# The softmax's output, from sub-block nine on, is transposed by way of DRAM and VectorE instead of TensorE

## The chip, the core and the metric

The kernel runs on one core of one Trainium2 chip. The metric is the device time of one launch in microseconds (us), as the median of several runs. The engines are TensorE (PE, matmuls and transposes), VectorE (DVE), ScalarE (ACT), GpSimd (POOL) and SyncE (SP); the sixteen DMA engines move data between DRAM and the on-chip SBUF. Each engine takes its instructions strictly in the order in which they were emitted for it, and waits at an instruction until what it reads is there.

## What is computed

Windowed attention over 4 batches of 8 heads, 576 positions, 64 values per head, then two feed-forward layers over the 2304 tokens, all in float32:

```python
scores = scale * np.matmul(q, k.transpose(0, 1, 3, 2))
rel = pos[:, None] - pos[None, :]
scores = np.where((rel >= 0) & (rel < 64), scores, -1e9)
attn = np.exp(scores - np.max(scores, axis=-1, keepdims=True))
attn = attn / (np.sum(attn, axis=-1, keepdims=True) + 1e-09)
x = np.matmul(attn, v)                    # then heads side by side: [2304, 512]
h = x @ w1_in; g = np.maximum(h, 0.0)**2; x = g @ w1_out       # first layer
h = x @ w2_in                                                   # second layer
P = a[0] + a[1]*h + a[2]*h**2 + a[3]*h**3
Q = 1.0 + np.abs(b[0])*np.abs(h) + np.abs(b[1])*h**2
out = (P / (Q + 1e-06)) @ w2_out
```

## The kernel before

**Tiling.** The 2304 tokens are 18 sub-blocks of 128, called i = 0 to 17 here (sub-block nine is i = 8), and five blocks of 512 (the last has 256). Attention is done by sub-block, in two halves (gl = 0, 1) of 64 queries for each of 8 heads; the layers are done by block, in 16 steps j over the 2048 hidden columns. Every weight product is split into a high and a low part, so it needs three matmuls. A step has 12 matmuls into h (`h_mm`, L619), the activation (`mid1`: ScalarE's relu and squares, VectorE's subtraction into g at L692), and 12 matmuls of g into four accumulators (`out_mm`, L638), one step later.

**Where attention lies.** While the first layer works on block b, the sub-blocks of block b + 1 go through attention in slots between its matmuls: `q` and `k` (transposes of the inputs; from i = 12 on VectorE does them in 32x32 squares from data that was rearranged in DRAM, L463 and L485), `s` (the scores, L525, both halves, followed by `softmax`), `p` (the transposes of the softmax's output, one slot per half) and `x` (the values matmuls, L585). Scores of sub-block i + 1 and values of i are joined into one step on TensorE (`sx`).

**The route of a half.** VectorE masks the scores and takes the maximum (L542), ScalarE takes exponentials and sums (L547), VectorE inverts the sums (L551, L552) and multiplies (L555) into the tile `sm`. `slot_p` transposes `sm` on TensorE, four 128x128 pieces against the identity into PSUM (L568), and ScalarE or VectorE copies them into the tile `pT` (L573). The values matmuls read `pT` and v. There are two `sm` tiles and two `pT` tiles, used in turn.

**What sets the order.** Nothing is issued while the program is written: each piece is an `Item` with an assumed duration per engine, and `Plan.run` takes, one after the other, the item that can start earliest (ties by due time) and emits it. So an engine's order follows from the assumed durations, and from assumed gaps between engines (`Plan.gap`: 2000 ns after a DMA). Loads and stores are issued by SyncE (L319, `load`), all in one queue. GpSimd makes the masks and multiplies for i = 0 to 3, and after that does nothing.

## Time and profile before

| | us |
|---|---|
| median of 3 runs (lowest, highest) | 886.32 (885.85, 887.77) |
| the profiled execution | 890.21 |
| its span in the trace | 888.4 |
| TensorE busy | 870.5 |
| VectorE busy | 674.3 |
| ScalarE busy | 561.0 |
| GpSimd busy | 11.5 |

The profiled execution is one more run, with the profiler on; between its span and its time lie 1.8 us outside the trace. The first layer with the attention takes the first half of the span, the second layer the rest. In the profile's rows, "out<-in" are the names of the tiles, with their numbers left out, PEld is TensorE's loading of the stationary operand, and "idle before" is the time that the engine stood before the instruction, with the engine and line that let it go.

### The profile page before, as it was taken

The numbers are of one execution on the slowest core, as the hardware profiler recorded it, in microseconds if no ns is written. First come the engines' busy times: TensorE is split into PE (matmuls) and PEld (weight loads), VectorE is DVE, ScalarE is ACT, GpSimd is POOL, SyncE is SP. The second block draws the span as 40 slices with busy tenths as digits, with TensorE's granted clock in tenths as the row PEclk, the third lists the DMA queues.
The fourth block names the chain that finished last, engine by engine and source line by source line (L and its number), as shares of the span: only waits on it lengthen the run. The fifth ranks groups of instructions, "written<-read, shape, count | busy, mean of one in ns | idle before, by whom it ended". The sixth has DMA issues, their size and how long they took to land.

```text
span 888.4 us, 14088 instructions
## 1 busy us (share of the span) xinstructions
PE 870.5 (98%) x5152; PEld 726.5 (82%) x5152; DVE 674.3 (76%) x1435; ACT 561.0 (63%) x1172; POOL 11.5 (1%) x25
## 2 busy tenths in 40 slices
PE   7799999999999999999999999999999999999998
PEld 6678788888878888888899888888888888988886
DVE  6999995666466676754421899999999999999994
ACT  6778774656456554535444766676667667888764
POOL 4000000000000000000000000000000000000000
PEclk9999999999999999999999999999999999999999
DMA  9686662688855453633189910210011002100001
GB/s 230 187 243 199 188 192 84 200 219 220 223 179 184 147 184 141 238 134 126 49 313 372 361 45 0 96 48 1 1 47 48 1 1 94 49 1 24 1 1 48
DMA packets 152998, 113.64 MB, mean 128 GB/s; under 512 B 92769, under 2 KB 131681, under 8 KB 150881
## 3 DMA queue, kind: packets, MB, share of 16 engines
q1 hardware_dynamic: 152928, 112.75, 41.0%
q8 instruction: 40, 0.66, 0.3%
q14 instruction: 30, 0.24, 0.1%
HBM read 81.79 MB, written 34.08 MB: 130 GB/s over the span
## 4 chain that ended last, share of the span: by engine, by line
PE 88%; DVE 6%; DMA 3%; ACT 2%; issue 1%; SPq 0%; POOLq 0%; POOL 0%; ACTq 0%; DVEq 0%
PE h L619 30%; PE acc L640 22%; PE acc L638 19%; PE t L619 11%; PE t L525 1%; DMA raw<-in_moe_w_out_dram 1%; PE t L568 1%; DVE cvr L404 1%; PE h L585 1%; DVE cvr L407 1%; DVE sm L542 1%; DVE g L692 1%; DMA ld<-in_q_dram 0%; PE t L585 0%; DMA raw<-in_moe_w_in_dram 0%
## 5 line engine op out<-in xcount | busy, mean ns | idle before, releaser
L638 PE MATMUL acc<-g,wo 128*128 128x512 f32 (+1 forms) x960 | 215.9, 372 | 0.8 <-DVE g L692 0.8
L638 PEld LDWEIGHTS acc<-g,wo 128*128 128x128 f32 x960 | 167.3, 189 | 31.5 <-DVE g L692 1.4
L619 PE MATMUL h<-xh,wih 128*128 128x512 f32 (+1 forms) x480 | 181.1, 377 | 2.0 <-DVE rs L551 2.0
L619 PE MATMUL h<-xl,wih 128*128 128x512 f32 (+1 forms) x480 | 178.0, 371 | 0.3 <-DVE xl L603 0.3
L619 PE MATMUL h<-xh,wil 128*128 128x512 f32 (+1 forms) x480 | 178.3, 371 | 0.0
L619 PEld LDWEIGHTS h<-xh,wih 128*128 128x128 f32 x480 | 91.0, 190 | 18.0 <-ACT sm L547 2.1
L692 DVE TENSOR_TENSOR g<-cvr,g 128x512 fp32r<-128x512 f32 (+1 forms) x80 | 50.8, 635 | 71.7 <-ACT cvr L690 71.4
L619 PEld LDWEIGHTS h<-xh,wil 128*128 128x128 f32 x480 | 91.1, 190 | 16.0 <-DVE wil L419 0.4
L619 PEld LDWEIGHTS h<-xl,wih 128*128 128x128 f32 x480 | 91.1, 190 | 14.9 <-DVE xl L603 0.6
L685 ACT ACTIVATE cvr<-h 128x512 f32<-128x512 f32 (+1 forms) x80 | 44.3, 554 | 84.9 <-PE h L619 83.0
L640 PE MATMUL acc<-wo,cvr 128*128 128x512 f32 x384 | 93.1, 390 | 0.0
L640 PE MATMUL acc<-wo,g 128*128 128x512 f32 x384 | 93.1, 389 | 0.0
L640 PEld LDWEIGHTS acc<-wo,g 128*128 128x128 f32 x384 | 71.6, 188 | 14.6
L640 PEld LDWEIGHTS acc<-wo,cvr 128*128 128x128 f32 x384 | 71.5, 188 | 14.4
L736 DVE SCALAR_TENSOR_TENSOR kT<-kT,b,sm 128x512 f32<-128x512 f32 (+1 forms) x80 | 55.8, 698 | 16.4 <-ACT kT L731 13.8
L399 ACT ACTIVATE cvr<-raw 128x512 f32<-128x512 f32 x64 | 42.9, 671 | 30.3 <-DMA raw<-in_moe_w_out_dram 13.7
L738 ACT ACTIVATE raw<-kT,cb 128x512 f32<-128x512 f32 (+1 forms) x80 | 54.9, 686 | 8.8 <-DVE kT L736 6.6
L619 PE MATMUL t<-xl,wih 128*128 128x512 f32 (+1 forms) x160 | 58.9, 368 | 0.0
L619 PE MATMUL t<-xh,wil 128*128 128x512 f32 (+1 forms) x160 | 58.8, 368 | 0.0
L619 PE MATMUL t<-xh,wih 128*128 128x512 f32 (+1 forms) x160 | 58.8, 367 | 0.0
L749 DVE SCALAR_TENSOR_TENSOR pT<-pT,coef,raw 128x512 f32<-128x512 f32 (+1 forms) x80 | 55.8, 697 | 1.7
L740 ACT ACTIVATE raw<-raw,cb 128x512 f32<-128x512 f32 (+1 forms) x80 | 54.5, 681 | 1.7
(150 smaller groups left out, 1322.6 us busy)
## 6 DMA issues: line engine op xcount, KB each, us to landing
raw<-in_moe_w_in_dram SPq DMA_DIRECT2D x64, 256.0 KB, 3.4
raw<-in_moe_w_out_dram SPq DMA_DIRECT2D x32, 512.0 KB, 4.5
w2h_d<-raw SPq DMA_DIRECT2D x32, 256.0 KB, 2.1
w2l_d<-cvr SPq DMA_DIRECT2D x32, 256.0 KB, 2.1
ld<-in_v_dram SPq DMA_DIRECT2D x25, 256.0 KB, 3.9
out_dram<-ld SPq DMA_DIRECT2D x18, 256.0 KB, 2.1
x2h_d<-xh SPq DMA_DIRECT2D x4, 1024.0 KB, 5.1
x2l_d<-xl SPq DMA_DIRECT2D x4, 1024.0 KB, 7.7
```

What stands on the lines that cost most here:

```text
L399: plan.add({"act": act(DM)}, lambda e: A.activation(out=t.t, in_=raw.t.bitcast(F32)[:, :, 1], func=ACTF.Copy, scale=2.0 ** -112), [raw], [t])
L404: plan.add({"dve": dve(DM)}, lambda e: V.scalar_tensor_tensor(out=u(t), in0=u(t), scalar=3, in1=raw.t[:, :, 1], op0=ALU.logical_shift_left ...
L407: plan.add({"dve": dve(DM)}, lambda e: V.scalar_tensor_tensor(out=u(t), in0=raw.t[:, :, 0], scalar=29, in1=u(t), op0=ALU.logical_shift_rig ...
L619: T.matmul(out=v4(hp.t, n), lhsT=w.t[:, (c ^ 2) * 128:((c ^ 2) + 1) * 128], rhs=x.t[:, :n // 128, c, :], start=(c == 0 and z == 0), stop=( ...
L638: T.matmul(out=v4(acc[l, bi, m].t, n), lhsT=w.t[:, m, :], rhs=y.t[:, :n // 128, :], start=st, stop=en)
L640: T.matmul(out=v4(acc[l, bi, m].t, DM), lhsT=y.t[:, m, :], rhs=w.t, start=st, stop=en)
L685: plan.add({"act": act(n, True)}, lambda e: A.activation(out=r.t[:, :n], in_=hp.t[:, :n], func=ACTF.Relu), [hp], [r])
L692: plan.add({"dve": dve(n)}, lambda e: V.tensor_tensor(out=gl.t[:, :nq], in0=v4(r.t, n), in1=gh.t[:, :nq].bitcast(F32), op=ALU.subtract), [ ...
L736: plan.add({"dve": dve(n, ptr=1)}, lambda e: V.scalar_tensor_tensor(out=f(h2), in0=f(h2), scalar=b1, in1=f(ab), op0=ALU.mult, op1=ALU.add) ...
L738: plan.add({"act": act(n, ptr=1)}, lambda e: A.activation(out=f(y), in_=f(h2), func=ACTF.Ln, scale=2.0 ** -63, bias=cb[:, 0:1]), [h2], [y])
L740: plan.add({"act": act(n, ptr=1)}, lambda e: A.activation(out=f(y), in_=f(y), func=ACTF.Exp, scale=-1.0, bias=cb[:, 1:2]), [y], [y])
L749: plan.add({"dve": dve(n, ptr=1)}, lambda e: V.scalar_tensor_tensor(out=f(u), in0=f(u), scalar=coef[:, 0:1], in1=f(y), op0=ALU.subtract, o ...
```

## The change

From i = 8 on (`NPD`, the sub-blocks of the first two blocks) `slot_p` has no TensorE step and no PSUM tile. Instead, right after the multiplication, GpSimd issues a DMA that stores the half's [128, 512] tile into DRAM (`p_d`), and four DMAs that load it back into the same `sm` tile, so that partition 32 z + j holds key group z of query j of each 32. Now each 32x32 square only has to be transposed within itself, which VectorE does in one instruction into `pT`. For this the reductions, exponentials and multiplications of these sub-blocks write their tile in another layout (key group, head pair, 32 keys), and the values matmuls read their 64 columns as two pieces of 32. There are three `sm` tiles. An item can now carry its own gap (`lag`), and the two kinds of DMAs get durations on GpSimd of 1000 and 2500 ns and gaps of 3000 and 3500 ns.

```diff
@@ -42,6 +42,7 @@
         self.engines, self.emit, self.due = engines, emit, due
         self.deps, self.users = {}, []
         self.end = None
+        self.lag = None
 
 
 class Plan:
@@ -102,7 +103,8 @@
         def opened(it):
             it.ready = {}
             for e in it.engines:
-                it.ready[e] = max([d.end + self.gap(d.on, e) for d in it.deps], default=0)
+                it.ready[e] = max([d.end + (self.gap(d.on, e) if d.lag is None else d.lag) for d in it.deps],
+                                  default=0)
                 open_[e].append(it)
 
         for it in self.items:
@@ -176,6 +178,7 @@
     orders = (list(range(NB)), list(range(NB - 2)) + [NB - 1, NB - 2])
     NS0 = blocks[0][1] // 128
     NPE = sum(n for _, n in blocks[:3]) // 128
+    NPD = sum(n for _, n in blocks[:2]) // 128
     scale = 1.0 / float(D) ** 0.5
 
     ctx.enter_context(tc.manual_schedule())
@@ -194,7 +197,7 @@
     SMALL = [("cb", 2), ("coef", 6), ("na", 4), ("b1", 1)] + [(f"{x}{i}", 4) for x in ("nm", "su", "rs") for i in range(4)]
     TAGS = ([("ident", [128, 128], F32), ("mask", [128, 2, 128], F32)] +
             [(f"kT{i}", [128, HP, W + 128], F32) for i in range(2)] + [(x, [128, n], F32) for x, n in SMALL] +
-            [("pad", [128, 224], F32)] +
+            [("pad", [128, 208], F32)] + [("sm2", [128, 4, 128], F32)] +
             [(f"wi{x}{j}", [128, DM], F32R) for j in range(NF) for x in "hl"] +
             [(f"wo{j}", [128, KT, 2, 2, 128], F32R) for j in range(NF // 2)] +
             [(f"x{x}{i}", [128, 4, KT, 128], F32R) for i in range(2) for x in "hl"] +
@@ -232,6 +235,9 @@
     sq_d = {x: dram.tile([128, HP, (NSUB - NPE) * 4, 32], F32, name=f"{x}_squares_d") for x in "kq"}
 
 
+    p_d = dram.tile([NSUB - NPD, 2, 128, 4, 128], F32, name="p_d")
+
+
     turn = {}
 
     def buf(place, shape, dtype=F32, pool=sb, view=None):
@@ -255,7 +261,7 @@
 
     ALL_PS = ("t0", "h0", "t1", "h1", "acc0", "acc1", "acc2", "acc3")
     LD, RAW, CV = ring("ld", 6), ring("raw", 3), (0, 1, 2)
-    KTP, QTP, SM, PT = ring("kT", 2), ring("qT", 2), ring("sm", 2), ring("pT", 2)
+    KTP, QTP, SM, PT = ring("kT", 2), ring("qT", 2), ring("sm", 3), ring("pT", 2)
     shared = {}
 
     def part(place, tag, shape, dtype, view, gen=0):
@@ -313,11 +319,14 @@
 
     nat = {}
 
-    def load(dst, pieces, size, slow=1, reads=(), due=None):
+    def load(dst, pieces, size, slow=1, reads=(), due=None, own=None):
         def emit(_):
             for o, i in pieces():
-                nc.sync.dma_start(out=o, in_=i)
-        return plan.add({"dma": size / 360 * slow}, emit, reads, [dst], due)
+                (P if own else nc.sync).dma_start(out=o, in_=i)
+        it = plan.add({"pool": own[0]} if own else {"dma": size / 360 * slow}, emit, reads, [dst], due)
+        if own:
+            it.lag = own[1]
+        return it
 
     def toks(t0, n):
         done = 0
@@ -536,15 +545,25 @@
         sm[i, gl] = t
         kind = int((2 * i + gl) % GPB == 0)
         nm, su, rs = (buf(ring(x, 4), [128, 4]) for x in ("nm", "su", "rs"))
+        if i >= NPD:
+            keys = lambda x: x.rearrange("p (k j) -> p k j", j=32)
+            head = lambda c: t.t.rearrange("p k (h j) -> p k h j", j=32)[:, :, c, :]
+            full = lambda: t.t.rearrange("p k (h j) -> p k h j", j=32)
+            sums = lambda: rs.t.unsqueeze(1).unsqueeze(3).to_broadcast([128, 4, 4, 32])
+        else:
+            keys = lambda x: x
+            head = lambda c: t.t[:, c, :]
+            full = lambda: t.t
+            sums = lambda: rs.t.unsqueeze(2).to_broadcast([128, 4, 128])
 
         def top(_):
             for c in range(4):
-                V.tensor_tensor_reduce(out=t.t[:, c, :], in0=ps.t[:, c, :], in1=mask[:, kind, :], scale=-scale,
+                V.tensor_tensor_reduce(out=head(c), in0=keys(ps.t[:, c, :]), in1=keys(mask[:, kind, :]), scale=-scale,
                                        scalar=-NEG, op0=ALU.add, op1=ALU.min, accum_out=nm.t[:, c:c + 1])
 
         def exp(_):
             for c in range(4):
-                A.activation(out=t.t[:, c, :], in_=t.t[:, c, :], func=ACTF.Exp, scale=-1.0, bias=nm.t[:, c:c + 1],
+                A.activation(out=head(c), in_=head(c), func=ACTF.Exp, scale=-1.0, bias=nm.t[:, c:c + 1],
                              accum_out=su.t[:, c:c + 1])
 
         def norm(_):
@@ -552,16 +571,27 @@
             V.reciprocal(out=rs.t, in_=rs.t)
 
         def mul(e):
-            (P if e == "pool" else V).tensor_tensor(out=t.t, in0=t.t, in1=rs.t.unsqueeze(2).to_broadcast([128, 4, 128]),
-                                                    op=ALU.mult)
+            (P if e == "pool" else V).tensor_tensor(out=full(), in0=full(), in1=sums(), op=ALU.mult)
 
         plan.add({"dve": 850}, top, [ps], [t, nm])
         plan.add({"act": 1550}, exp, [nm, t], [t, su])
         plan.add({"dve": 350}, norm, [su], [rs])
         plan.add({"pool": 1400} if i < NS0 else {"dve": 690}, mul, [rs, t], [t])
+        if i >= NPD:
+            d = p_d[i - NPD, gl]
+            b = Buf(plan, f"p_d{i}{gl}", None)
+            load(b, lambda: [(d, t.t)], 1 << 18, reads=[t], own=(1000, 3000))
+            load(t, lambda: [(t.t[z * 32:(z + 1) * 32], d[:, z, :].rearrange("(a j) f -> j a f", j=32))
+                             for z in range(4)], 1 << 18, reads=[b], own=(2500, 3500))
 
     def slot_p(i, n, due):
-        src, ps = sm[i, n], ps_buf()
+        src = sm[i, n]
+        if i >= NPD:
+            t = pT[i, n] = buf(PT, [128, 4, 128])
+            plan.add({"dve": dve(512)}, lambda e: V.transpose(
+                t.t.rearrange("p a f -> p (a f)"), src.t.rearrange("p a f -> p (a f)")), [src], [t], due)
+            return
+        ps = ps_buf()
 
         def tr(_):
             for c in range(4):
@@ -585,7 +615,8 @@
                         T.matmul(
                             out=ps.t[e * 64:(e + 1) * 64, hp, gl * W:(gl + 1) * W],
                             lhsT=vg[gl].t[:, 2 * hp + e, :],
-                            rhs=pt[gl].t[:, hp, (e ^ gl) * 64:((e ^ gl) + 1) * 64],
+                            rhs=(pt[gl].t[:, (e ^ gl) * 2:(e ^ gl) * 2 + 2, hp * 32:(hp + 1) * 32] if i >= NPD else
+                                 pt[gl].t[:, hp, (e ^ gl) * 64:((e ^ gl) + 1) * 64]),
                             start=True, stop=True,
                         )
 
```

What the planner makes of it, at three places. Names before "<-" are written, names behind it read; numbers tell buffers apart.

TensorE, in the second block's steps at i = 13, before (h: `h_mm`, acc: `out_mm`, t from ident and sm: the transposes of the second half):

```order
L619 MATMUL h_3286<-xh_2107,wih_1117 128x512
L619 MATMUL h_3286<-xl_2114,wih_1117 128x512
L619 MATMUL h_3286<-xh_2107,wil_1124 128x512
L568 MATMUL t_3305<-ident,sm_3177 128x128 x4
L638 MATMUL acc_3031<-g,wo_1000 128x512 x3
L638 MATMUL acc_3039<-g,wo_1000 128x512 x3
L638 MATMUL acc_3044<-g,wo_1000 128x512 x3
L638 MATMUL acc_3050<-g,wo_1000 128x512 x3
```

and the same step now:

```order
L650 MATMUL h_3285<-xh_2122,wih_1119 128x512
L650 MATMUL h_3285<-xl_2135,wih_1119 128x512
L650 MATMUL h_3285<-xh_2122,wil_1126 128x512
L669 MATMUL acc_3019<-g,wo_1002 128x512 x3
L669 MATMUL acc_3026<-g,wo_1002 128x512 x3
L669 MATMUL acc_3032<-g,wo_1002 128x512 x3
L669 MATMUL acc_3051<-g,wo_1002 128x512 x3
```

The four transposes are gone, and the accumulating matmuls follow the step's last h matmul directly. Over the program TensorE has 2863 rows where it had 2883.

GpSimd, at the end of its work before (multiplications for i = 1 to 3, whose halves lie in weight tiles):

```order
L555 TENSOR_TENSOR wil_358<-wil_358,rs_412 128x512
L555 TENSOR_TENSOR wih_373<-wih_373,rs_453 128x512
L555 TENSOR_TENSOR wil_415<-wil_415,rs_487 128x512
L555 TENSOR_TENSOR wih_517<-wih_517,rs_557 128x512
L555 TENSOR_TENSOR wil_526<-wil_526,rs_585 128x512
L884 UNCONDITIONAL_BRANCH
L884 ISA
```

and now, the rows for i = 13 and 14 out of 40 new ones (p_d: the tensor in DRAM; x4: the four loads of a half):

```order
L325 DMA p_d<-sm_3167 128x512
L325 DMA p_d<-sm_3182 128x512
L325 DMA sm_3167<-p_d 32x4x128 x4
L325 DMA sm_3182<-p_d 32x4x128 x4
L325 DMA p_d<-sm_3399 128x512
L325 DMA p_d<-sm_3422 128x512
L325 DMA sm_3399<-p_d 32x4x128 x4
L325 DMA sm_3422<-p_d 32x4x128 x4
```

Both stores of a sub-block are issued ahead of both halves' loads; this is the order for all but i = 16, where the first half's loads stand ahead of the second store.

VectorE, after the multiplications for i = 13, before (raw, cvr: conversions of the second layer's weights; g: the activation's subtraction):

```order
L401 TENSOR_SCALAR raw_3246<-raw_3246 128x512
L404 SCALAR_TENSOR_TENSOR cvr<-cvr,raw_3246 128x512
L407 SCALAR_TENSOR_TENSOR cvr<-raw_3246,cvr 128x512
L419 TENSOR_TENSOR cvr<-cvr,raw_3246 128x512
L691 TENSOR_TENSOR cvr<-cvr 128x512
L401 TENSOR_SCALAR raw_3291<-raw_3291 128x512
L692 TENSOR_TENSOR g<-cvr,g 128x4x128
L404 SCALAR_TENSOR_TENSOR cvr<-cvr,raw_3291 128x512
L407 SCALAR_TENSOR_TENSOR cvr<-raw_3291,cvr 128x512
L419 TENSOR_TENSOR cvr<-cvr,raw_3291 128x512
```

and now:

```order
L410 TENSOR_SCALAR raw_3256<-raw_3256 128x512
L413 SCALAR_TENSOR_TENSOR cvr<-cvr,raw_3256 128x512
L416 SCALAR_TENSOR_TENSOR cvr<-raw_3256,cvr 128x512
L428 TENSOR_TENSOR cvr<-cvr,raw_3256 128x512
L591 STREAM_TRANSPOSE pT_3327<-sm_3167 128x512
L410 TENSOR_SCALAR raw_3294<-raw_3294 128x512
L723 TENSOR_TENSOR g<-cvr,g 128x4x128
L413 SCALAR_TENSOR_TENSOR cvr<-cvr,raw_3294 128x512
L416 SCALAR_TENSOR_TENSOR cvr<-raw_3294,cvr 128x512
L591 STREAM_TRANSPOSE pT_3348<-sm_3182 128x512
```

The two square transposes stand on both sides of a subtraction into g, 11 and 16 rows behind the second multiplication of the same sub-block, and wait there for the loads.

## Rows read from the trace of the kernel before

**Rows 1.** The page: span; busy us, share and instructions of each engine

```profile
span 888.4 us, 14088 instructions
PE 870.5 (98%) x5152; PEld 726.5 (82%) x5152; DVE 674.3 (76%) x1435; ACT 561.0 (63%) x1172; POOL 11.5 (1%) x25
```

**Rows 2.** The page: chain that ended last, by engine, then by line

```profile
PE 88%; DVE 6%; DMA 3%; ACT 2%; issue 1%; SPq 0%; POOLq 0%; POOL 0%; ACTq 0%; DVEq 0%
PE h L619 30%; PE acc L640 22%; PE acc L638 19%; PE t L619 11%; PE t L525 1%; DMA raw<-in_moe_w_out_dram 1%; PE t L568 1%; DVE cvr L404 1%; PE h L585 1%; DVE cvr L407 1%; DVE sm L542 1%; DVE g L692 1%; DMA ld<-in_q_dram 0%; PE t L585 0%; DMA raw<-in_moe_w_in_dram 0%
```

**Rows 3.** Stretches: length, busy PE PEld DVE ACT POOL, clock, DMA share, GB/s

```profile
145.00:258.00 113.00, 110.83 (x727) 90.22 (x726) 72.05 (x189) 66.16 (x167) 0.00 (x0) 0.99 0.71 194
258.00:346.00 88.00, 88.00 (x585) 71.98 (x584) 54.71 (x141) 48.63 (x115) 0.00 (x0) 0.99 0.59 192
```

**Rows 4.** By line, 145:440 us, PE: count, busy us, mean ns, idle

```profile
L568 PE MATMUL t<-ident,sm 128*128 128x128 f32 x80 | 12.0, 272 | 2.1 <-DVE sm L555 2.1
```

**Rows 5.** Timeline, PE, around one slot: start us, us, what

```profile
219.78 0.39 PE L619 MATMUL h<-xh,wil 128*128 128x512 f32 x1
220.02 0.60 PE L568 MATMUL t<-ident,sm 128*128 128x128 f32 x4
220.37 0.48 PE L619 MATMUL h<-xh,wih 128*128 128x512 f32 x1
220.69 0.40 PE L619 MATMUL h<-xl,wih 128*128 128x512 f32 x1
```

**Rows 6.** Timeline, PE: twelve weight matmuls, then scores and values

```profile
216.61 2.88 PE L638 MATMUL acc<-g,wo 128*128 128x512 f32 x12
219.33 0.39 PE L619 MATMUL h<-xh,wih 128*128 128x512 f32 x1
...
268.67 1.10 PE L525 MATMUL t<-kT,qT 64*64 64x128 f32 x32
269.70 1.15 PE L585 MATMUL h<-pT,ld 128*64 128x64 f32 x32
```

**Rows 7.** Instructions by line, whole span, DVE, shapes apart

```profile
L401 DVE TENSOR_SCALAR raw<-raw 128x512 uint32<-128x512 uint32 x64 | 27.1, 424 | 20.1 <-ACT cvr L399 19.6 <-DMA ld<-in_v_dram 0.3 <-DMA w2h_d<-raw 0.2
L692 DVE TENSOR_TENSOR g<-cvr,g 128x512 fp32r<-128x512 f32 x64 | 44.0, 688 | 36.8 <-ACT cvr L690 36.6
L463 DVE STREAM_TRANSPOSE qT<-ld 128x512 f32<-128x512 f32 x6 | 4.3, 710 | 3.9 <-DMA ld<-q_squares_d 3.9
L483 DVE COPY kT<-kT 128x256 f32<-128x256 f32 x6 | 1.7, 280 | 0.0
```

**Rows 8.** Timelines, DVE and PE: a subtraction and the matmuls that read it

```profile
300.84 0.69 DVE L692 TENSOR_TENSOR g<-cvr,g 128x512 fp32r<-128x512 f32 x1
...
302.64 0.62 PE L638 MATMUL acc<-g,wo 128*128 128x512 f32 x2
```

**Rows 9.** Timeline, DVE: the multiplications of the scores of 268.67

```profile
275.46 0.65 DVE L555 TENSOR_TENSOR sm<-sm,rs 128x512 f32<-128x512 f32 x1
...
276.90 0.69 DVE L555 TENSOR_TENSOR sm<-sm,rs 128x512 f32<-128x512 f32 x1
```

**Rows 10.** DMA issues: engine, count, KB each, median us from issue to landing

```profile
w2h_d<-raw SPq DMA_DIRECT2D x32, 256.0 KB, 2.1
...
ld<-q_squares_d SPq DMA_DIRECT2D x6, 256.0 KB, 3.2
```

**Rows 11.** Timeline, SP: four DMA issues in a row

```profile
130.72 2.54 SPq L319 DMA_DIRECT2D k_squares_d<-in_k_dram  x4
```

**Rows 12.** Timeline, POOL: its last operation

```profile
26.55 1.04 POOL L555 TENSOR_TENSOR wil<-wil,rs 128x512 f32<-128x512 f32 x1 [0.59 <-DVE rs L552]
```

**Rows 13.** Timeline, PE: the wait before a slot

```profile
255.76 0.63 PE L568 MATMUL t<-ident,sm 128*128 128x128 f32 x4 [2.10 <-DVE sm L555]
```

**Rows 14.** Stretches behind that wait, columns as in rows 3

```profile
256.00:258.00 2.00, 2.00 (x9) 1.67 (x8) 1.97 (x6) 1.57 (x3) 0.00 (x0) 0.63 0.00 0
258.00:260.00 2.00, 2.00 (x6) 1.54 (x5) 2.00 (x4) 1.85 (x4) 0.00 (x0) 0.51 0.92 385
```

## The prediction, made before the changed kernel was run

> **What bounds the kernel now.** I read the table of busy times first, then the chain of work that ended last, then the stretches of the stage that changes, and there the timelines. TensorE is busy 98% of the span, VectorE 76%, ScalarE 63%, GpSimd 1% [rows 1]. The chain runs 88% through TensorE, and the transposes that the change removes (L568) have 1% of it, weight matmuls 30, 22 and 19% [rows 2]. What matters is that TensorE has nearly no holes where the change acts: of 145 to 258 us it works 110.8 of 113, of 258 to 346 all 88, while VectorE has a third of each stretch free (72.1 and 54.7 us busy) [rows 3]. An instruction taken off TensorE there is therefore worth its own length, and a wait put on TensorE costs its own length. No other engine's busy time counts, only whether it delivers late.
>
> **What goes.** For i = 8 to 17, ten sub-blocks with two halves each, 20 slots of four transposes leave TensorE (80 instructions, x80 in [rows 4]). Their busy time, 12.0 us, is an upper bound, for matmuls overlap. What a slot costs is read from the spacing around it: the last matmul before it starts at 219.78 and the second one after it at 220.69, 0.91 us for two matmuls which elsewhere stand 0.2267 apart (twelve from 216.61 to 219.33) [rows 5, 6]. So a slot costs 0.91 - 0.45 = 0.46 us, and 20 slots **9.2 us**. That is the gain, if nothing else arrives late. The 20 evictions of PSUM go too; they lie on ScalarE and VectorE beside TensorE, so I count nothing.
>
> **What comes, off the path.** VectorE gets 20 square transposes at 0.71 us [rows 7], 14.2 us, covered by its idle third; where the cover is gone, one of them delays the g subtraction behind it (L692). The tightest such place I found has 0.69 us of subtraction from 300.84 and its matmul at 302.64, 1.1 us of slack [rows 8], so one transpose that does not wait for its data fits. The transfers add 20 times 512 KB of write and read, on DMA engines that are 0.71 and 0.59 busy [rows 3]. Reductions, exponentials and values matmuls now walk in pieces of 32 elements; no row shows these pieces. Zero is my value, since the weight matmuls also read x in pieces and keep their pace; a doubled values step (1.15 us, ten times, [rows 6]) is the far end, 11.5 us, and I give it almost no chance.
>
> **What comes, on the path.** A half's route is now: multiply (L555), store, four loads, square transpose, values matmul. TensorE meets the values at a place fixed by the order, and behind them, in order, stand all weight matmuls. So the sum is a race between two lengths.
>
> Available. In the changed order 81 to 87 weight matmuls lie between scores i and values i for i = 8 to 15, against 75 to 96 before. Take 84 at 0.2267: 19.0 us. With the scores itself (1.03, from 268.67 to 269.70), the previous values (1.15) and the next scores (1.03) [rows 6] that is 22.2 us; for i = 11 and 15 no scores follow, 21.2. The first multiply ends 7.4 us after the scores start (275.46 + 0.65 against 268.67) [rows 6, 9]. What is left is **14.8 us** for six sub-blocks, 13.8 for two. For i = 16 and 17 there are 189 and 120 matmuls, 43 and 27 us, and no race.
>
> Needed. GpSimd issues store 0, store 1, loads 0 (four), loads 1 (four) in this order, so from the first multiply to the second half's data pass one store issue, a landing, eight load issues and a landing. The second store's issue falls into the first one's landing; the second multiply ends 1.5 us after the first [rows 9]. A 256 KB store lands in 2.1 us, a 256 KB load of 32-wide squares in 3.2 [rows 10], and the transpose takes 0.71. Sum: 9c + 6.0 us, where c is what GpSimd needs for one DMA. No row shows c. Nearest from below is the same operation on SyncE: four issues in 2.54 us, 0.63 each [rows 11]; nearest from above is GpSimd's own 128x512 operation, 1.04 us [rows 12]. With 0.63 the need is 11.7 us, with 1.04 it is 15.4. I take the lower part, since SyncE's row is the same work on another engine, and then nobody waits: margin 3.1 and 2.1 us. At the upper end six sub-blocks wait 0.6 and two 1.6 us, together 6.8, and 2.4 us of gain are left.
>
> The Trainium skill, "DMA: Bandwidth & Descriptors", section "Latency and other measured facts", puts the first byte of a GpSimd-issued DMA at about 1 us and of one from SyncE at about 0.6. By that page each of the two landings would be some 0.4 us later, an estimate: the need 12.5 us, still inside. No run here shows it yet.
>
> **A wait that may go.** At 255.76 TensorE stood 2.10 us for the multiply of i = 12, directly before the removed transposes [rows 13], and then had a granted clock of 0.63 and 0.51 for four microseconds, the lower of its two levels (1.2 of 2.4 GHz) for most of them [rows 14]: another 0.43 x 4 = 1.7 us. So 3.8 us hang on it. The order removes the waiting instruction, but the block's eviction and g subtraction stand in the same VectorE queue at 254 to 258 us and would be late next. Bounds 0 to 3.8; I take zero, as the next waiter needs the same VectorE work.
>
> **Sum.** The profiled execution took 890.21 us for a span of 888.4; it lies 3.9 above the median of the three runs, 886.32. The change is a difference within the span, -9.2 + 0 = -9.2, so against the median the forecast is **877.1 us**. With the boundary wait gone wholly it would be 873.3; with c at its upper row 883.9.
>
> **Rivals.** (A) GpSimd is slow at issuing. The mechanism is the race above, its place the values of i = 8 to 15. It turns into a loss where the waits eat 9.2 us: 6x + 2(x + 1) = 9.2, x = 0.9, so c = (14.8 + 0.9 - 6.0)/9 = 1.08 us, hardly above GpSimd's row of 1.04. At c = 1.2 the need is 16.8: six waits of 2.0 and two of 3.0, 18 us, net +8.8, **895 us**; if each of them costs the clock as the one at 255.76 did, eight times 1.7 more, 909. For it: GpSimd issued no DMA before, and its rows are the slowest of all engines for their size. Against it: nothing in the trace says that an issue costs as much as an elementwise operation.
>
> (B) VectorE holds GpSimd off. VectorE has operations that run in a faster form: 512 elements in 0.424 us (L401) where L692 takes 0.69, and a copy of 256 in 0.28 [rows 7]. Between the first multiply and the second transpose of i = 13 the order has two of L401's and one copy, 1.1 us. If GpSimd stands still for them the need is 12.8 to 16.5 us: nothing at the lower end, 1.7 and 2.7 us at the upper one, 15.6 in all, net +6.4, **893 us**. The Trainium skill, "SBUF — State Buffer", section "SBUF: two separate sides", speaks of this against the change: while VectorE runs in a two-port mode, GpSimd cannot write descriptors, and such a DMA waits. By that rule the answer is (B); whether these rows are such a mode, and whether it matters, no run here shows yet.
>
> (C) The gain is given back through VectorE's queue. The first transpose of a half stands before a g subtraction and cannot be overtaken. Its data need 5c + 5.3 us from the multiply, 8.5 to 10.5. The rows between hold some 6.5 us of VectorE work and two subtractions, which TensorE's step spaces 5.4 us apart (24 matmuls), so they pass after 6.5 to 9 us. A wait of 2 us in each of eight sub-blocks would leave 0.9 beyond the 1.1 us of slack, 7.2 in all: **884 us**. That the change does not do what it says is out: the order has 20 rows fewer on TensorE.
>
> **How the numbers follow.** Forecast (873 to 882): 0.50, because the lower price is the like operation. (C), 882 to 888: 0.20. (A): 0.23, since its point of decision is so near to GpSimd's own row. (B): 0.07. A measurement of this kernel tells 0.2%, 1.8 us, from no change. Faster by more: all of the forecast and 0.11 of (C), 0.61. Slower by more: 0.21 of (A) and 0.06 of (B), 0.27. Between: 0.12. The range goes from the boundary wait gone, 873, up into (A) as far as c of about 1.2 with part of the clock's cost, 902; about 0.04 lie below it and 0.11 above.
>
> **What would show it.** Right: no transposes on TensorE between 145 and 440 us, TensorE with no waits at the values line, GpSimd's eight loads of a pair within 5 to 8 us, the stage from 145 to 440 shorter by 9 us and the rest alike. (A): waits of TensorE on the transpose line or of VectorE on the loaded tile, equal in every sub-block from 8 to 15, and a granted clock below 1 after them. (B): issue times on GpSimd that differ with what VectorE runs. (C): the g subtraction as TensorE's waited-for line. The forecast is wrong above all if c is over 1.08 us, which only the result can tell.

## The result: 0.6% slower, though the gain is there

| | before | changed |
|---|---|---|
| median of 7 runs, us | 886.55 | 892.17 |
| lowest to highest | 885.85 to 888.02 | 888.73 to 894.55 |
| profiled execution; its span | 890.21; 888.4 | 894.55; 892.3 |

The ratio is 1.0057, with a 95% interval of 1.0038 to 1.0076: 5.1 us slower, 3.4 to 6.7. The forecast was 877.1; the range, up to 902, took the time in, but the direction was wrong.

The page of the changed kernel, as [rows 1]: TensorE's busy time fell by 4.1 us and the span grew by 3.9, so that TensorE now stands still for 892.3 - 866.4 = 25.9 us instead of 17.9.

```profile
span 892.3 us, 14161 instructions
PE 866.4 (97%) x5072; PEld 722.1 (81%) x5072; DVE 682.5 (76%) x1450; ACT 552.9 (62%) x1157; POOL 67.8 (8%) x125
```

The stretches of [rows 3], with the same columns (length, busy PE PEld DVE ACT POOL, granted clock, DMA share, GB/s). Before, TensorE worked 110.83 and 88.00 us of them; the DMA share was 0.71 and 0.59:

```profile
145.00:258.00 113.00, 107.61 (x681) 86.62 (x680) 72.49 (x189) 60.21 (x155) 22.49 (x41) 0.97 0.84 232
258.00:346.00 88.00, 84.18 (x550) 68.39 (x550) 60.47 (x153) 46.96 (x112) 22.56 (x40) 0.98 0.71 217
```

TensorE's timeline there and up to 445 us, its six longest waits (start, us, instruction, [idle before <- releaser]): four values matmuls, at i = 10, 11, 12 and 15, wait for a square transpose (L591), and two groups of out matmuls for a g subtraction. At i = 8, 9, 13, 14, 16 and 17 the values do not wait.

```profile
211.42 1.03 PE L615 MATMUL h<-pT,ld 128*64 128x64 f32 x28 [1.41 <-DVE pT L591]
228.94 2.80 PE L669 MATMUL acc<-g,wo 128*128 128x512 f32 x11 [0.89 <-DVE g L723]
236.43 1.76 PE L615 MATMUL t<-pT,ld 128*64 128x64 f32 x28 [2.24 <-DVE pT L591]
276.10 1.14 PE L615 MATMUL h<-pT,ld 128*64 128x64 f32 x28 [2.29 <-DVE pT L591]
343.52 1.03 PE L615 MATMUL t<-pT,ld 128*64 128x64 f32 x28 [1.10 <-DVE pT L591]
384.92 2.81 PE L669 MATMUL acc<-g,wo 128*128 128x512 f32 x11 [1.22 <-DVE g L723]
```

The two waits over 2 us, at i = 11 and i = 12, are followed by the lower clock level (0.50), as the one of [rows 13, 14] was. Stretches of two microseconds, columns as above:

```profile
237.00:239.00 2.00, 2.00 (x26) 1.79 (x23) 0.77 (x2) 1.25 (x2) 0.00 (x0) 0.50 0.77 220
239.00:241.00 2.00, 2.00 (x6) 1.52 (x6) 1.88 (x4) 0.89 (x2) 0.00 (x0) 0.50 0.76 226
...
278.00:280.00 2.00, 2.00 (x6) 1.51 (x6) 2.00 (x15) 1.55 (x5) 0.00 (x0) 0.50 0.57 161
```

Who is late? GpSimd's instructions by line (count, busy us, mean ns, idle before) and the DMA issues of the page (KB each, median us from issue to landing), the latter as [rows 10]:

```profile
L325 POOL DMA_DIRECT2D sm<-p_d x80 | 44.9, 565 | 35.6 <-DMA p_d<-sm 32.0 <-DVE cvr L428 1.5 <-issue 1.0
```

```profile
w2h_d<-raw SPq DMA_DIRECT2D x32, 256.0 KB, 3.4
...
p_d<-sm POOLq DMA_DIRECT2D x20, 256.0 KB, 3.9
sm<-p_d POOLq DMA_DIRECT2D x80, 64.0 KB, 4.3
```

GpSimd issues a DMA in 0.56 us, below my lower bound of 0.63. The landings are late: 3.9 us where I had taken 2.1, 4.3 where I had 3.2. SyncE's own transfers land later too: the w2h_d store of [rows 10] went from 2.1 to 3.4 us.

Not every wait for a square transpose is a wait for a landing. At i = 10, 12 and 15 VectorE itself stood for the loaded tile before the second transpose (2.08, 3.40 and 1.75 us). At i = 11 it did not. It stood for ScalarE, which had stood 3.17 us for one of SyncE's raw loads, and came to the second transpose through its other work without a pause (timeline, DVE):

```profile
232.02 0.43 DVE L410 TENSOR_SCALAR raw<-raw 128x512 uint32<-128x512 uint32 x1 [3.14 <-ACT cvr L408]
...
235.67 0.70 DVE L591 STREAM_TRANSPOSE pT<-sm 128x512 f32<-128x512 f32 x1
```

From 145 to 445 us TensorE waits 10.3 us in all. Of these, 1.41 + 2.29 + 1.10 = 4.8 ended with a landing of the new transfers; the other 5.5 did not.

### The profile page after: what moved, and what is told of

It reads as the page before. It is cut to its first block, busy times and chain, and to the rows that moved or that the text cites. A ratio compares the mean times of both kernels' runs of the same rounds, so it can differ in the third digit from the quotient of the medians.

```text
span 892.3 us, 14161 instructions
## 1 busy us (share of the span) xinstructions
PE 866.4 (97%) x5072; PEld 722.1 (81%) x5072; DVE 682.5 (76%) x1450; ACT 552.9 (62%) x1157; POOL 67.8 (8%) x125
## 4 chain that ended last, share of the span: by engine, by line
PE 58%; DMA 2%; ACT 1%; DVE 1%; issue 0%; SPq 0%; ACTq 0%; DVEq 0%
PE acc L671 22%; PE h L650 17%; PE t L650 11%; PE acc L669 7%; DMA raw<-in_moe_w_in_dram 1%; DMA raw<-in_moe_w_out_dram 1%; DMA sm<-p_d 0%; ACT sm L566 0%; PE t L615 0%; PE t L534 0%; DVE g L723 0%; ACT raw L427 0%; SPq L325 0%; PE h L615 0%; DVE xl L738 0%
```

## The experiments

The kernel before took 886.6 to 889.4 us in the groups of runs, so all times below are ratios to it within the group, turned into us at 886.5; "changed" is +5.1. A difference between two rows carries the uncertainty of both, some 2 to 3 us.

| kernel | difference, us | 95% interval |
|---|---|---|
| changed | +5.1 | +3.4 to +6.7 |
| no transfers | -9.8 | -12.2 to -7.3 |
| SyncE's traffic cut | -10.4 | -12.3 to -8.4 |
| two of SyncE's stores cut | -1.1 | -2.4 to +0.4 |
| transfers, nobody waits | -2.8 | -4.0 to -1.7 |
| gaps of 5000 and 6000 | +11.9 | +9.7 to +14.2 |
| all gaps as measured | -0.4 | -1.6 to +0.9 |
| without i = 11, 12 | +2.7 | +1.4 to +3.8 |
| only i = 16, 17 | -0.1 | -1.3 to +1.2 |
| i = 12 to 17 | +1.1 | -0.1 to +2.2 |
| i = 12 to 17, gaps as measured | -3.6 | -4.9 to -2.4 |
| before, with a gap of 3500 | -1.1 | -2.1 to -0.1 |

**Is the gain there?** The transfers are left out.

```diff
-            for o, i in pieces():
+            for o, i in pieces() if not own else ():
...
```

> The changed kernel without GpSimd's transfers (the store to p_d and the four loads of each half are left out, so the squares are transposed without having been rearranged). Every other engine has the instructions of the changed kernel in the same order. Theory (the gain of 9.2 us is there and is eaten by transfers that land too late, and by the clock behind the waits): no wait of TensorE for VectorE's square transpose (L591), 875 to 879 us, that is 8 to 11 below the kernel before, and the other DMAs land as in the kernel before. Rival (the gain never was there, because pieces of 32 elements in softmax and values, or the changed order, cost it): 887 us or more, as slow as the changed kernel to within 4 us.

Measured: 878.23 us, -9.8. The theory holds for the time. The page shows 5072 matmuls and transposes, as in the changed kernel, but less busy time (9.6 us less, at a mean granted clock of 1.000 instead of 0.990; 1.5 of these lie before 145 us, where no transfer runs yet) and 7.6 us less idleness.

```profile
span 875.1 us, 13926 instructions
PE 856.8 (98%) x5072; PEld 715.9 (82%) x5072; DVE 682.2 (78%) x1450; ACT 553.0 (63%) x1157; POOL 11.5 (1%) x25
```

One wait for a square transpose is left, 1.32 us, again at i = 11, although nothing is transferred. It was not expected. Here too VectorE had stood 2.95 us for ScalarE, and ScalarE 2.97 us for a raw load:

```profile
229.91 1.03 PE L615 MATMUL t<-pT,ld 128*64 128x64 f32 x28 [1.32 <-DVE pT L591]
```

So more than half of the changed kernel's 2.24 us at i = 11 belongs to the new order, not to the transfers. SyncE's stores land nearly as before for w2h_d (2.3 us), later for w2l_d (3.1 instead of 2.1).

Two more things can be read. The pieces of 32 elements cost nothing: an exponential takes 389 ns in the median before and after the change, a multiplication 684 and 683, the values matmuls of a sub-block 1.15 us. And VectorE's busy time, 682.2 us here against 682.5 in the changed kernel, shows that GpSimd's issues do not slow it.

**Is it SyncE's traffic, or GpSimd's way of issuing?** SyncE's loads and stores for the second layer's weights become slivers.

```diff
+                f = 16 if l and j > 1 else 256
+                return [(o[:, c ^ 2:(c ^ 2) + 2, :f], i[:, c:c + 2, :f]) for c in (0, 2)]
...
-                load(w2_b[j, io, x], lambda p=p, d=d: [(d[io, j], p().bitcast(F32))], 1 << 18, reads=[b], due=due)
+                load(w2_b[j, io, x], lambda p=p, d=d, f=16 if j > 1 else DM: [(d[io, j][:, :f], p().bitcast(F32)[:, :f])], 1 << 18, reads=[b], due=due)
...
```

> The changed kernel with all its transfers on GpSimd and the same order on the compute engines, but SyncE's traffic cut: for the conversion of the second layer's weights (from its third tile on) only slivers of 16 or 32 columns are loaded and stored, and the second layer reads one stored tile again and again, so its result is not the layer's. Theory (GpSimd's transfers land late because they share the sixteen DMA engines with SyncE's stores and loads): store and loads of a half land in 2.0 to 2.7 us instead of 3.9 and 4.3, VectorE's waits for the loaded tile vanish, and the time is 875 to 881 us. Rival (a DMA that GpSimd issues lands late by itself): landings stay near 4 us, the waits of 2.2 us at i = 11 and i = 12 stay, 888 us or more.

Measured: 878.24 us, -10.4, with all of GpSimd's transfers in place. The time came out as the theory had it, the landings not quite: 3.1 us each in the median, still above the 2.7. TensorE's only wait for a square transpose between 145 and 445 us is one of 1.1, once more at i = 11. No run cut this traffic in the kernel before, so the time by itself does not say how much of the gain SyncE's own shorter traffic makes.

The transfers by themselves, in a kernel of their own:

> The transfers by themselves: a 256 KB store to DRAM and four loads of 64 KB of 32-wide squares, four times each (1) issued by GpSimd with nothing beside, (2) by SyncE with nothing beside, (3) by GpSimd while SyncE streams 512 KB loads, (4) by SyncE while ScalarE streams the same loads. Nothing of the reference is computed. Theory (shared DMA engines): alone both engines land in 2.0 to 2.5 us for the store and 2 to 3.2 us for the loads, equal to 0.4 us; beside the stream both are longer by 1.5 us or more. Rival (GpSimd's own DMAs are slow): phase 1 is longer than phase 2 by 1.5 us or more on each landing.

DMA issues of its four phases in order (engine's queue, count, KB each, median us to landing): alone by GpSimd and by SyncE, then beside a stream, by GpSimd and by SyncE.

```profile
pd<-half POOLq DMA_DIRECT2D x4, 256.0 KB, 2.3
half<-pd POOLq DMA_DIRECT2D x16, 64.0 KB, 2.2
...
pd<-half SPq DMA_DIRECT2D x4, 256.0 KB, 2.0
half<-pd SPq DMA_DIRECT2D x16, 64.0 KB, 2.0
...
pd<-half POOLq DMA_DIRECT2D x2, 256.0 KB, 5.8
half<-pd POOLq DMA_DIRECT2D x8, 64.0 KB, 5.7
...
half<-pd SPq DMA_DIRECT2D x16, 64.0 KB, 3.8
pd<-half SPq DMA_DIRECT2D x3, 256.0 KB, 6.0
```

Alone, GpSimd's transfers land 0.3 and 0.2 us later than SyncE's; beside a stream both need 1.8 to 4.0 us more, whoever issues them. Alone, then, the engine that issues hardly counts; what the DMA engines already have to do counts. (The loads' 5.7 against 3.8 us beside the stream do not compare the two engines: the stream kept the DMA engines full in the third phase, but only 0.5 to 1.0 busy in stretches of the fourth.) The Trainium skill, "DMA: Bandwidth & Descriptors", section "Latency and other measured facts", gives a memory latency of 0.2 us on average and 2 us at high load, as the largest part of a transfer's fixed cost: the direction agrees, but the 3.5 us more that GpSimd's transfers need here are more than that row gives.

**Which traffic?** i = 12's transfers have the longest landings, and two 1 MB stores of SyncE are issued beside them. Here these two write 64 KB each.

```diff
+            r = 1 if bi == 1 else None
-            load(x2_b[bi, x], lambda x=x: [(x2_d[x][:, t0 // 128:(t0 + n) // 128], xs[x].t[:, :n // 128].bitcast(F32))], n << 11,
+            load(x2_b[bi, x], lambda x=x, r=r: [(x2_d[x][:, t0 // 128:(t0 + n) // 128][:, :r, :r], xs[x].t[:, :n // 128].bitcast(F32)[:, :r, :r])], n << 11,
...
+        t0 = blocks[0][0] if bi == 1 else t0
```

> The changed kernel, but the two 1 MB stores that SyncE issues at 261 and 262 us (x2h_d and x2l_d of the block that has just ended) write 64 KB each; the second layer later reads the stored input of another block in their place. All orders are unchanged. Theory (i = 12's transfers, 8.1 us in the median and up to 9.0, are slow because of these two stores): they land in 4 to 5 us, the wait of 2.29 us at 276 us and the lower clock behind it go, some 4 us below the changed kernel, that is 0 to 2 us above the kernel before. Rival (the raw loads and the stores of converted weights beside them are enough): landings of i = 12 stay above 6 us, the wait stays, 4 to 6 us above the kernel before.

Measured: -1.1, so 6.2 us below the changed kernel, with an uncertainty of some 2 that just reaches the 4 expected. TensorE's wait at i = 12 and the lower clock behind it are gone, and the theory holds. The DMA issues of the place in the changed kernel (255 to 275 us):

```profile
x2h_d<-xh SPq DMA_DIRECT2D x1, 1024.0 KB, 4.9
x2l_d<-xl SPq DMA_DIRECT2D x1, 1024.0 KB, 8.7
...
sm<-p_d POOLq DMA_DIRECT2D x8, 64.0 KB, 8.2
raw<-in_moe_w_in_dram SPq DMA_DIRECT2D x2, 256.0 KB, 10.2
```

and with the two stores cut (250 to 270 us):

```profile
raw<-in_moe_w_in_dram SPq DMA_DIRECT2D x2, 256.0 KB, 3.0
...
sm<-p_d POOLq DMA_DIRECT2D x8, 64.0 KB, 2.7
```

The loads land 5.5 us sooner, and the raw loads beside them 7.2 us. The kernel of transfers alone moved 414 GB/s while its stream kept the DMA engines full (a stretch of it: length, busy DVE ACT POOL, granted clock, DMA share, GB/s):

```profile
69.00:74.00 5.00, 0.00 (x0) 0.00 (x0) 0.25 (x1) 1.00 1.03 414
```

At that rate 2.1 MB take 5.1 us (an estimate), about what the loads had lost, as if they stood behind the stores. In the run with SyncE's weight traffic cut, these two stores remain, and i = 12's loads still take 7.2 us in the median. But TensorE does not wait there: the stores make the landing long, and the last microsecond, which is too much, comes with the weight traffic. In the changed kernel VectorE stands for the loads twice, and the g subtraction behind it (timeline, DVE):

```profile
271.22 0.71 DVE L591 STREAM_TRANSPOSE pT<-sm 128x512 f32<-128x512 f32 x1 [4.21 <-DMA sm<-p_d]
275.33 0.71 DVE L591 STREAM_TRANSPOSE pT<-sm 128x512 f32<-128x512 f32 x1 [3.40 <-DMA sm<-p_d]
275.97 0.65 DVE L723 TENSOR_TENSOR g<-cvr,g 128x512 fp32r<-128x512 f32 x1
```

**Is it only the wait?** All transfers run, but the loads are issued behind the transpose.

```diff
+            if own and own[0] > 2000:
+                later[dst] = lambda: [P.dma_start(out=o, in_=i) for o, i in pieces()]
+                return
...
+            def square(_):
+                V.transpose(t.t.rearrange("p a f -> p (a f)"), src.t.rearrange("p a f -> p (a f)"))
+                later.pop(src)()
...
```

> The changed kernel with all its transfers, but each half's four loads are issued after VectorE's square transpose instead of before it (so the transpose reads the tile as it was before the way through DRAM, not rearranged). Each engine has the instructions of the changed kernel in the same order, but for GpSimd, where a load may stand behind a store; the traffic is the same, some microseconds later. Only the wait for the landing is gone. Theory (the wait for the transfer costs, the added traffic by itself next to nothing): no wait of TensorE for the square transpose beyond the 1.3 us that is also there without transfers, 876 to 881 us or 8 to 11 below the kernel before. Rival (the traffic holds up SyncE's loads and so costs time by itself): 884 us or more, with waits for other tiles.

Measured: 886.33 us, -2.8. My theory fell here: I had the traffic at next to nothing, and it alone takes back 9.8 - 2.8 = 7.0 us. The waiting for the landing takes 5.1 + 2.8 = 7.9 more. (The loads lie later here and so meet other traffic; with the intervals of the runs the split is good to some 3 us.) TensorE's waits in this kernel, two of the four:

```profile
194.13 1.12 PE L484 MATMUL t<-ident,ld 128*128 128x128 f32 x4 [2.35 <-DMA ld<-in_q_dram]
...
235.88 1.03 PE L622 MATMUL t<-pT,ld 128*64 128x64 f32 x28 [1.90 <-DVE pT L596]
```

The first is a load of q by SyncE that TensorE reads directly. The second transpose has its data, but stands in VectorE's queue behind the conversion of weights, which waits for ScalarE, which waits for a raw load. It is i = 11 again, where 1.32 us of this wait are there without transfers. All of TensorE's waits from 145 to 445 us make 5.6 us here, and 1.3 without transfers. ScalarE, then VectorE:

```profile
230.79 0.66 ACT L412 ACTIVATE cvr<-raw 128x512 f32<-128x512 f32 x1 [2.68 <-DMA raw<-in_moe_w_in_dram]
```

```profile
231.48 0.43 DVE L414 TENSOR_SCALAR raw<-raw 128x512 uint32<-128x512 uint32 x1 [2.64 <-ACT cvr L412]
...
235.12 0.70 DVE L596 STREAM_TRANSPOSE pT<-sm 128x512 f32<-128x512 f32 x1
```

That is general: ScalarE's waits for the larger raw loads between 145 and 445 us (total, times, longest) are, without transfers and in this kernel,

```profile
ACT cvr L408 <- DMA raw<-in_moe_w_out_dram: 12.7, 8, 3.2
```

```profile
ACT cvr L412 <- DMA raw<-in_moe_w_out_dram: 19.1, 9, 4.8
```

and the g of 384.92 in the changed kernel is late in the same way.

**Does more room help?** Two orders with larger assumed gaps.

```diff
-            load(b, lambda: [(d, t.t)], 1 << 18, reads=[t], own=(1000, 3000))
+            load(b, lambda: [(d, t.t)], 1 << 18, reads=[t], own=(600, 5000))
...
-                             for z in range(4)], 1 << 18, reads=[b], own=(2500, 3500))
+                             for z in range(4)], 1 << 18, reads=[b], own=(2250, 6000))
```

> The changed kernel in which the planner assumes other figures for GpSimd's transfers (600 ns and a gap of 5000 for the store, 2250 and 6000 for the loads), so that between the scores and the values of i = 8 to 15 there are 105, 99, 90, 93, 102, 93, 90 and 90 weight matmuls instead of 81 to 87: 1.4 to 4.8 us more room. Transfers and amount of work are unchanged. Theory (the need is about 14 us and up to 19 beside SyncE's traffic, against 13.8 to 14.8 of room): the waits at the values of i = 11 and i = 12 go, and with them the lower clock, 878 to 884 us. Rival (what costs is not the race but the added traffic or work): 888 us or more, waits elsewhere.

Measured: 900.44 us, +11.9, the worst of all: a miss, and as slow as the rival had it. The waits for the transposes are gone but for one of 0.5, as expected, and others came, seven microseconds of them for the eviction of the values (L634). At the first, ScalarE stood 9.07 us for a raw load with the eviction of the values (L633) queued behind it. That load landed in 4.2 us; but SyncE issued it only at 193.49 us, after issues of q's rearrangement that took 3.63 us. So it was late because it was issued late, not because the added traffic slowed it. ScalarE, then TensorE:

```profile
197.68 0.66 ACT L408 ACTIVATE cvr<-raw 128x512 f32<-128x512 f32 x1 [9.07 <-DMA raw<-in_moe_w_out_dram]
198.25 0.57 ACT L633 CAST xh<-h 128x512 fp32r<-128x512 f32 x1
```

```profile
199.59 0.50 PE L650 MATMUL h<-xh,wih 128*128 128x512 f32 x1 [2.31 <-DVE xl L634]
```

So with the gaps measured, for SyncE's loads too (600 and 4000, 2250 and 4500, and in `Plan.gap`):

```diff
-            return 2000
+            return 3500
```

> The changed kernel with the planner's assumptions set to what was measured: 600 ns and a gap of 4000 for a store, 2250 and 4500 for the loads, and a gap of 3500 instead of 2000 behind all of SyncE's DMAs. Between scores and values of i = 8 to 15 there are then 93, 87, 87, 93, 93, 99, 90 and 87 weight matmuls. Work and traffic are unchanged. Theory (an order made with true landings lets nobody wait): the waits at the values and those for SyncE's loads shrink to under 4 us in the two stretches from 145 to 346 us, 877 to 884 us. Rival (landings vary too much, 2 to 9 us, for any fixed figure, or more room moves the waits to the eviction of the values as in the kernel with gaps of 5000 and 6000): 888 us or more.

Measured: 888.87 us, -0.4: 5.5 us better than the changed kernel, but not the 877 to 884 expected. From 258 to 346 us TensorE works 87.15 of 88; between 145 and 258 it still waits 2.33 us for g and 3.45 for i = 11's transpose. That one stands in VectorE's queue behind ScalarE's wait of 5.17 us for a raw load, as in the changed kernel.

**Where can the route stand?**

> The changed kernel, but i = 11 and i = 12, which stood on TensorE's two longest waits (2.24 and 2.29 us, each with a lower clock behind it), keep the transposes on TensorE. Theory (the loss sits in these two places): 4 slots of 0.46 us come back, the waits and the clock behind them (4.5 + some 3.5 us) go, so about 6 us below the changed kernel, 884 to 888 us, at or below the kernel before. Rival (the waits belong to no sub-block but to whatever meets SyncE's traffic in the new order): waits appear at other sub-blocks, 889 us or more.

```diff
+    DRAM = [i for i in range(NPD, NSUB) if i not in (11, 12)]
...
-        if i >= NPD:
+        if i in DRAM:
...
```

Measured: 891.74 us, +2.7: the rival. TensorE's waits at i = 10 and i = 15, 1.41 and 1.10 us in the changed kernel, grow to 2.19 and 2.00, and at the block's boundary the wait of [rows 13] is back:

```profile
212.27 1.76 PE L616 MATMUL h<-pT,ld 128*64 128x64 f32 x28 [2.19 <-DVE pT L592]
...
258.32 0.63 PE L599 MATMUL t<-ident,sm 128*128 128x128 f32 x4 [2.39 <-DVE sm L575]
339.48 1.03 PE L616 MATMUL t<-pT,ld 128*64 128x64 f32 x28 [2.00 <-DVE pT L592]
```

The last two sub-blocks alone (`NPD` from `blocks[:4]`):

> Only the halves of i = 16 and 17 go through DRAM, with 189 and 120 weight matmuls between scores and values; all others stay on TensorE as in the kernel before. Theory (0.46 us per slot, no loss where the way has 27 us or more): 4 slots, 1.8 us below the kernel before, by 1 to 3, the place from 346 us on alone shorter. Rival (a transfer costs TensorE time wherever it runs): no difference or slower than before.

Measured: -0.1, where 1.8 were expected; the interval, to -1.3, leaves the theory's smallest gain open and its forecast out. The place shows where 0.8 of the 1.8 us go; the other 1.0 the times cannot tell from none. VectorE, then TensorE:

```profile
378.34 0.71 DVE L591 STREAM_TRANSPOSE pT<-sm 128x512 f32<-128x512 f32 x1 [2.43 <-DMA sm<-p_d]
378.98 0.65 DVE L723 TENSOR_TENSOR g<-cvr,g 128x512 fp32r<-128x512 f32 x1
```

```profile
379.68 2.79 PE L669 MATMUL acc<-g,wo 128*128 128x512 f32 x11 [0.78 <-DVE g L723]
```

TensorE reads this transpose much later, but VectorE's order has it early, and the g behind it is needed at once.

At last the route for i = 12 to 17, with measured gaps and with the changed kernel's own, and the kernel before with the gap of 3500 alone:

```diff
-    NPD = sum(n for _, n in blocks[:2]) // 128
+    NPD = sum(n for _, n in blocks[:3]) // 128
```

> The way through DRAM only for i = 12 to 17, where the DMA engines have more room (0.71 busy from 258 to 346 us in the changed kernel, against 0.84 from 145 to 258), with the planner's assumptions as measured (600 and 4000, 2250 and 4500, 3500 behind SyncE's DMAs): 93, 93, 90 and 87 weight matmuls between scores and values of i = 12 to 15. Theory (the loss is made where the DMA engines are nearly full): 12 slots of 0.46 us, 5.5 us, and the wait at the block's boundary (2.1 and some 1.7 of clock) go, one or two waits of 1 us come: 4 to 8 us below the kernel before. Rival (a transfer costs others as much as it saves wherever SyncE converts weights): within 1.5 us of the kernel before.

> The same choice of sub-blocks, i = 12 to 17, with the changed kernel's own assumptions: 93, 93, 84 and 87 weight matmuls between scores and values. Theory (the place decides, not the assumed gaps): 3 to 8 us below the kernel before, at most 3 us above the run with measured assumptions. Rival: within 1.5 us of the kernel before or slower.

> The kernel before with a gap of 3500 instead of 2000 assumed behind SyncE's DMAs and nothing else: what the new order is worth without the way through DRAM. Theory: it has no part in the result, within 1.5 us of the kernel before. Rival: it is faster by 2 us or more, and what the runs with measured assumptions gain is the order's, not the route's.

Measured: 885.61 us, -3.6, with measured gaps: faster than both kernels, if a little less than expected. With the changed kernel's own gaps +1.1 (the rival), and the kernel before with the gap alone -1.1. So neither the place nor the gaps suffice by themselves, and what the route adds to the gaps is some 2.5 us, give or take 2. In the fast version the wait at the block's boundary is gone, and of the waits from 145 us on the two longest are

```profile
272.56 1.03 PE L615 MATMUL h<-pT,ld 128*64 128x64 f32 x28 [1.76 <-DVE pT L591]
...
307.06 2.80 PE L669 MATMUL acc<-g,wo 128*128 128x512 f32 x11 [0.75 <-DVE g L723]
```

where the first is i = 12 beside the two stores again; with the changed kernel's own gaps that wait was 3.31.

## Why the prediction was wrong

**The gain, 9.2 us: right in size.** Without transfers the kernel gains 9.8 (7.3 to 12.2). The wait at the boundary, which I took as staying late, is missing in the changed kernel and in the fast version, and there (2.39 us) in the run that leaves i = 12 on TensorE. My reason, that the next waiter needs the same VectorE work, holds in one run: with i = 12 to 17 and the changed kernel's own gaps, TensorE waits 1.51 us for g at 257.35. Slots and boundary together give 13.0; less the 1.32 us that the new order waits at i = 11 without transfers this is 11.7, inside the interval.

**GpSimd's issue, c: right, and not the danger.** 0.56 us lie outside my bounds of 0.63 to 1.04 on the good side, so rival (A) could not occur. (B) neither: the 80 load issues take 548 ns at least, 551 in the median and 857 at most, though VectorE is busy 64 to 69% of those stretches.

**The landings: the step that failed.** I took 2.1 and 3.2 us from medians of SyncE's rows over the whole span, which count quiet stretches too, as if the new transfers would not meet anyone. They measured 3.9 and 4.3. The need is then 9 x 0.56 + 3.9 + 4.3 + 0.7 = 13.9 us instead of 11.7, and the margins of 3.1 and 2.1 shrink to 0.9 and nothing. The waits at i = 10 and i = 15 (1.41 and 1.10 us) ended with such a landing. The long one at i = 11 did not: its 2.24 us came through a raw load and VectorE's queue, and 1.32 of them are there without transfers. At i = 12 the loads need 8.2 and up to 9.0 us: 9 x 0.56 + 2.3 (its store) + 9.0 + 0.7 = 17.0, so 2.2 beyond the room of 14.8, and TensorE waited 2.29. Two stores that I had not looked for set this; without them the kernel is 6.2 us faster, give or take 2. So the sum's conclusion, "then nobody waits", fell for three sub-blocks of eight by this mis-sized term.

**The traffic: a term without a price.** I noted 20 times 512 KB on DMA engines that were 0.71 and 0.59 busy, and set nothing for it in the sum. This is the second step that failed. By the run in which nobody waits for the data it costs 7.0 us, give or take 3, through SyncE's loads of q and of raw weights.

**The room: measured at the wrong engine.** "For i = 16 and 17 no race" counted to TensorE's values. VectorE's transpose stands much earlier in its queue than TensorE needs it, and g behind it. That is rival (C)'s mechanism, which I had at i = 8 to 15 alone, with a chance of 0.20; the run with i = 16 and 17 alone shows it with 0.78 us. In the changed kernel neither of the two waits for g shown above is of this kind. That at 384.92 comes from a raw load. Before that at 228.94 VectorE runs none of the new transposes between 211.4 and 233.1 us; its g waits for ScalarE, which had stood 5.26 us for a raw load at 223.66.

**The clock: right in kind.** In the changed kernel the lower level follows the two waits of over 2 us, as I had it for (A). Not every such wait has it: after the 2.33 us for g, at 229.63 in the run with all gaps as measured, the granted clock stayed at 1.00. The changed kernel's TensorE is busy 9.6 us longer than the one without transfers for the same instructions, 1.5 of them before 145 us. The stretches at 0.50 to 0.73 from 235 to 243 and from 277 to 281 us cost some 4.7 us (an estimate from clock and length), of 17.2 us between the two spans; the rest of the longer busy time was not traced. The two spans are single executions, the changed one the slowest of its seven; by the ratios the two kernels are 14.9 us apart.

## What to carry to other kernels

A transfer's landing time belongs to the stretch in which it will run, not to the transfer: read it there, name the largest transfers of the other queues nearby, and add what they hold divided by the rate at full DMA engines. Where the DMA engines are as busy as here (0.71 before the change), price new traffic for the loads of others as well, and measure the room up to the first in-order engine that waits, not up to the last reader. Before an order is made from assumed latencies, set them to measured ones for all queues: larger figures for one queue alone made it worse here. And before a wait is put down to a landing, look whether the engine that does the work stood for the data, or came late from other work.

## What was not expected of the hardware

- A 64 KB load landed in 2.2 us alone, in 4.3 in this kernel, and in 8.2 behind two 1 MB stores of another queue, and a 256 KB store in 2.3 and 5.8 us beside a stream: queues of different engines are not independent of each other.
- GpSimd issues a DMA in 0.56 us, whether VectorE works or not; SyncE's issue of the same store took 0.34 in the kernel of transfers alone.
